# Holding the later loads of a fused attention and feed-forward kernel back until the second token tile's statistics are done

## The chip, the cores and the metric

The kernel runs on one core of a Trainium2 chip. The metric is the device time of one execution in microseconds (us); lower is better. Times are compared only within a job, that is, on one chip. Traces of different jobs come from different chips, so a difference between two of them can be one of the chips. In the engine names of the profile, PE is TensorE, PEld its weight loads, DVE is VectorE, ACT is ScalarE, POOL is GpSimd and SP is SyncE, which issues most of the DMAs.

## The reference, cut to what matters

Layer norm of 2048 tokens by 576 features, then linear attention (32 heads of 18) and a GEGLU feed-forward part (4608 wide) side by side on the same normalized input, both added to the input.

```python
x = A_x                                   # 1 x 2048 x 576, bf16
xn = _layernorm(x, axis=-1)
# attention: qkv = xn @ wqkv (576 x 1728); phi(q), phi(k); kv and z over all tokens; num / den; @ wo
# feed-forward: (gelu(xn @ w_gate) * (xn @ w_up)) @ w_down
return x + _A_ref(xn, A_wqkv, A_wo) + _B_ref(xn, B_w_gate, B_w_up, B_w_down)
```

Only the first 15 us matter here: the first token tiles of `x` and the K third of `wqkv` have to arrive, the tiles have to be normalized and transposed, and then TensorE can begin with the K projection and need not stop again for half a millisecond.

## The kernel before

The sixteen token tiles of `x` come in six loads, the K, Q and V thirds of the QKV weights in a load each, with a small load for the last 64 of their 576 rows. K goes through ScalarE's queue, everything else through SyncE's.

```python
def load_x(n0, cnt):
    nc.sync.dma_start(x_sb[:, n0:n0 + cnt, :], x_view[:, n0:n0 + cnt, :])

def load_w(which, on=nc.sync):
    c = slice(which * D, (which + 1) * D)
    on.dma_start(wqkv_sb[:, 0:4, c], A_wqkv[0:512, c].rearrange("(kt p) c -> p kt c", p=P))
    on.dma_start(wqkv_sb[0:HP, 4, c], A_wqkv[512:576, c])
    if which == 0:
        on.dma_start(wq_lo[HP:P, :], A_wqkv[512:576, c])
# ...
load_x(0, 1)
load_x(1, 1)
load_x(2, 2)
# ...
nc.vector.memset(wqkv_sb[0:1, 0, D:D + 2], 0.0)
load_w(1, nc.scalar)                      # K
```

The rest of the start is a list of steps, each with a time that only orders them. The statistics of tiles 0 and 1 stand at 3.15 and 4.09, the first normalization at 5.03. The loads of x 4 to 7, of the Q weights and of x 8 to 15 hang on a write of two elements into x tile 4: the load overwrites them, so SyncE has to wait for the write, and its queue is in order.

```python
todo += [(t, spin, count) for t, count in [(5.80, 3), (6.20, 5), (8.50, 2)]]   # filler matmuls

todo += [(4.0, lambda n: nc.vector.memset(x_sb[0:1, n, 0:2], 0.0), 4)]
todo += [(4.01, lambda n: load_x(n, 4), n) for n in (4,)]
todo += [(4.02, lambda n: load_w(0), 0)] + [(4.03, lambda n: load_x(n, 4), n) for n in (8, 12)]
todo.sort(key=lambda x: x[0])
```

`spin` multiplies an identity matrix by itself into an unused bank, so that TensorE is not idle between the first transposes.

## Time and profile before

| | before |
|---|---|
| time, median of the first 3 runs | 523.75 us (523.57 to 524.0) |
| span of the profiled run | 521.7 us, granted clock 1.0 |
| K weights issued, landed | 1.95, 7.37 us |
| TensorE's first K projection | 7.41 us, after 0.79 us of waiting |
| x 4 to 7: issue, first packet | 4.25, 5.66 us |

The lines behind this table stand in the prediction below. Where it or I speak of a first packet or of bytes at a time, they are counted from the trace's packet records by queue and packet size: packets of 4608 bytes are x 4 to 15, of 2304 bytes x 2 and 3, and q10 carries the K weights alone.

### The profile page before, as it was taken

The page shows a single profiled execution, that of the slowest core. Times are in us where ns is not written, and L with a number is a line of the kernel's source. Part 1 is how long each engine was busy: PE and PEld are TensorE (multiplying, and loading weights), DVE is VectorE, ACT ScalarE, POOL GpSimd, SP SyncE. Part 2 cuts the span into 40 slices and gives each one's busy share as a digit, 9 for nine tenths or more (in the row PEclk, how much of TensorE's full clock was granted, in tenths as well). Part 3 has the DMA queues.
Part 4 walks back from the last instruction along what each step waited for, and adds up shares of the span by engine and source line. Part 5 has one row for each costly group of instructions (what it writes and reads, how often), then busy time and mean ns, then how long its engine had stood idle before and what let it go on. Part 6 is the DMA issues. An engine that isn't in the chain of part 4 may idle for free.

```text
span 521.7 us, 10641 instructions
## 1 busy us (share of the span) xinstructions
PE 516.1 (99%) x4498; PEld 313.5 (60%) x4498; DVE 250.9 (48%) x436; ACT 143.1 (27%) x293; POOL 35.2 (7%) x55
## 2 busy tenths in 40 slices
PE   7999999999999999999999999999999999999997
PEld 6777755555587754444577744444777544445775
DVE  7996565876358323433388133333584233433101
ACT  6898442332320013323200032232000123322000
POOL 2021000211001100000012000000011000000000
PEclk9999999999999999999999999999999999999999
DMA  8334609899500045555300155555100355440000
GB/s 279 62 64 118 154 25 264 254 269 266 157 12 13 13 124 155 144 156 160 93 13 13 41 166 145 155 156 155 29 23 13 103 161 158 140 134 2 13 11 24
DMA packets 106282, 57.89 MB, mean 111 GB/s; under 512 B 13370, under 2 KB 105722, under 8 KB 106234
## 3 DMA queue, kind: packets, MB, share of 16 engines
q1 hardware_dynamic: 105626, 56.55, 38.8%
q8 instruction: 35, 0.57, 0.5%
q10 hardware_dynamic: 608, 0.66, 0.4%
q14 instruction: 13, 0.11, 0.1%
HBM read 52.86 MB, written 2.36 MB: 106 GB/s over the span
## 4 chain that ended last, share of the span: by engine, by line
PE 97%; DMA 1%; ACT 1%; DVE 0%; issue 0%
PE ps_all L313 55%; PE ps_all L677 27%; PE ps_all L289 4%; PE ps_all L682 4%; PE ps_all L245 3%; PE ps_all L342 3%; DMA wqkv_sb<-in_A_wqkv_dram 1%; PE ps_all L451 1%; PE ps_all L433 0%; PE ps_all L659 0%; ACT xnT L234 0%; ACT L114 0%; ACT phi_e L265 0%; ACT phi_e L269 0%; DVE hT L273 0%; DVE res L685 0%
## 5 line engine op out<-in xcount | busy, mean ns | idle before, releaser
L313 PE MATMUL ps_all<-xnT,wg 64*128 64x512 bf16 x1152 | 272.6, 376 | 0.0
L313 PE MATMUL ps_all<-xnT,wu 64*128 64x512 bf16 x1152 | 271.8, 376 | 0.0
L648 DVE TENSOR_TENSOR hT<-ps_all,gl 128x512 bf16<-128x512 f32 x144 | 99.5, 691 | 161.9 <-ACT gl L647 161.2
L647 ACT ACTIVATE gl<-ps_all 128x512 f32<-128x512 f32 x144 | 86.1, 598 | 314.3 <-PE ps_all L313 297.4
L313 PEld LDWEIGHTS <-wu 64*128 64x128 bf16 x1152 | 108.3, 94 | 66.3
L313 PEld LDWEIGHTS <-wg 64*128 64x128 bf16 x1152 | 108.3, 94 | 66.1
L677 PE MATMUL ps_all<-wd_sb,hT 128*128 128x288 bf16 x1152 | 147.0, 286 | 0.0
L677 PEld LDWEIGHTS <-hT 128*128 128x128 bf16 x1152 | 112.3, 98 | 30.6 <-issue 1.3
L475 DVE RECIPROCAL den_sb<-den_sb 126x128 f32<-126x128 f32 (+1 forms) x80 | 68.3, 911 | 0.5
L685 DVE TENSOR_TENSOR res<-ps_all,x_sb 128x288 bf16<-128x288 f32 x32 | 14.7, 458 | 88.0 <-PE ps_all L682 88.0
L313 PE MATMUL ps_all<-xnT,wr 64*128 64x512 bf16 x288 | 55.1, 376 | 0.0
L478 POOL TENSOR_TENSOR pqT<-pqT,den_sb 126x512 bf16<-126x512 bf16 (+3 forms) x25 | 24.2, 966 | 317.3 <-DVE den_sb L475 279.4
L682 PE MATMUL ps_all<-m_sb,pqT 126*128 126x288 bf16 (+1 forms) x160 | 24.9, 285 | 0.0
L313 PEld LDWEIGHTS <-wr 64*128 64x128 bf16 x288 | 14.4, 94 | 16.9 <-issue 0.7
L245 PE MATMUL ps_all<-wqkv_sb,xnT 128*128 128x288 bf16 x160 | 22.5, 286 | 0.9 <-DMA wqkv_sb<-in_A_wqkv_dram 0.8
L289 PE MATMUL ps_all<-hT,xn 128*128 128x288 bf16 (+4 forms) x176 | 22.4, 275 | 0.0
L289 PEld LDWEIGHTS <-xn 128*128 128x128 bf16 (+1 forms) x176 | 17.5, 102 | 4.1
L245 PEld LDWEIGHTS <-xnT 128*128 128x128 bf16 x160 | 15.4, 98 | 6.9 <-issue 1.4
L682 PEld LDWEIGHTS <-pqT 126*128 126x128 bf16 (+1 forms) x160 | 15.5, 97 | 4.1
L342 PE MATMUL ps_all<-xnT,wqkv_sb 128*126 128x512 bf16 (+1 forms) x70 | 17.4, 378 | 0.0
L273 DVE SCALAR_TENSOR_TENSOR hT<-ps_all,phi_e 128x288 bf16<-128x288 f32 x32 | 13.2, 450 | 4.6 <-ACT phi_e L269 4.0
L265 ACT ACTIVATE phi_e<-ps_all 128x288 f32<-128x288 f32 x32 | 12.9, 410 | 3.6 <-PE ps_all L245 2.1
(68 smaller groups left out, 173.8 us busy)
## 6 DMA issues: line engine op xcount, KB each, us to landing
wg<-in_B_w_gate_dram SPq DMA_DIRECT2D x72, 256.0 KB, 2.9
wu<-in_B_w_up_dram SPq DMA_DIRECT2D x72, 256.0 KB, 3.5
wd_sb<-in_B_w_down_dram SPq DMA_DIRECT2D x12, 432.0 KB, 4.6
wr<-in_B_w_gate_dram SPq DMA_DIRECT2D x72, 32.0 KB, 2.7
wr<-in_B_w_up_dram SPq DMA_DIRECT2D x72, 32.0 KB, 3.1
out_dram<-res SPq DMA_DIRECT2D x15, 144.0 KB, 1.8
x_sb<-in_A_x_dram SPq DMA_DIRECT2D x3, 576.0 KB, 7.1
wqkv_sb<-in_A_wqkv_dram SPq DMA_DIRECT2D x2, 576.0 KB, 4.7
```

Source lines behind the costliest of these rows:

```text
L245: nc.tensor.matmul(ps_all[:, k_bank(n, hf), :HALF], lhsT=xnT[:, kt, n * P:(n + 1) * P], rhs=wqkv_sb[:, kt, D + hf * HALF:D + (hf + 1) * HALF],
L273: nc.vector.scalar_tensor_tensor(out=out_, in0=ps, scalar=0.0, in1=e, op0=ALU.max, op1=ALU.add)
L289: nc.tensor.matmul(ps_all[:m, b, col:col + w], lhsT=xn[:, n, j0:j0 + m], rhs=pk[:, n, d0:d0 + w], start=(n == 0 and col == 0), stop=(n == ...
L313: return nc.tensor.matmul(self.outs[i], lhsT=self.lhs(i, rows, kt), rhs=self.rhs(i, rows, kt), start=start, stop=stop, skip_group_check=True,)
L342: nc.tensor.matmul(ps, lhsT=wqkv_sb[:, kt, q0:q0 + rows], rhs=xnT[:, kt, sc * SC:(sc + 1) * SC], start=(kt == 0), stop=(kt == KT - 1),)
L475: nc.vector.reciprocal(out=d[:, h:h + P], in_=d[:, h:h + P])
L478: nc.gpsimd.tensor_tensor(out=pqT[:rows, c, cols], in0=pqT[:rows, c, cols], in1=d, op=ALU.mult)
L647: nc.scalar.activation(out=gl[:], in_=ps_all[:, b[0], :], func=ACT.Gelu_apprx_tanh)
L648: nc.vector.tensor_tensor(out=hT[:, GUB * k + i, :], in0=ps_all[:, b[1], :], in1=gl[:], op=ALU.mult)
L677: nc.tensor.matmul(acc, lhsT=hT[:, f, j * P:(j + 1) * P], rhs=wd_sb[:, f, hs], start=(f == 0), stop=False,)
L682: nc.tensor.matmul(acc, lhsT=pqT[:rows, c, ts_], rhs=m_sb[:rows, c, hs], start=False, stop=(c == NCH - 1),)
L685: nc.vector.tensor_tensor(out=res[:, hs], in0=acc, in1=x_sb[:, n, hs], op=ALU.add)
```

## The change

The intent: the loads held back should come a microsecond later still, so that the K weights, which TensorE waits for, have the DMA engines to themselves.

```diff
-    todo += [(4.0, lambda n: nc.vector.memset(x_sb[0:1, n, 0:2], 0.0), 4)]
-    todo += [(4.01, lambda n: load_x(n, 4), n) for n in (4,)]
-    todo += [(4.02, lambda n: load_w(0), 0)] + [(4.03, lambda n: load_x(n, 4), n) for n in (8, 12)]
+    todo += [(5.0, lambda n: nc.vector.memset(x_sb[0:1, n, 0:2], 0.0), 4)]
+    todo += [(5.01, lambda n: load_x(n, 4), 4), (5.02, lambda n: load_w(0), 0)]
+    todo += [(5.03, lambda n: load_x(n, 4), n) for n in (8, 12)]
```

The write moves behind the second tile's statistics (4.09). No instruction is added or taken away on any engine, and only VectorE's order changes.

## The prediction

> **What bounds the kernel now.** I read the busy table and the chain of waits on the page first, then who waited for whom on TensorE, then the chain in order of time over the first 14 us, then the timelines of the engines there, and last the DMA queues in short stretches.
>
> From the page of the kernel before:
>
> ```profile
> PE 516.1 (99%) x4498; PEld 313.5 (60%) x4498; DVE 250.9 (48%) x436; ACT 143.1 (27%) x293; POOL 35.2 (7%) x55
> PE 97%; DMA 1%; ACT 1%; DVE 0%; issue 0%
> ```
>
> TensorE is busy for 99% of the span, and 97% of the chain that ended last is TensorE's own work. The 3% that is not (1% DMA, 1% ACT) is all a change to loads can reach. Who waited for whom on TensorE, over the whole run (what waited, for what: us in total, times, longest):
>
> ```profile
> PE ps_all L133 <- POOL ident masks.py:199: 1.4, 1, 1.4
> PE ps_all L245 <- DMA wqkv_sb<-in_A_wqkv_dram: 0.8, 1, 0.8
> PE ps_all L231 <- DVE xn L216: 0.3, 1, 0.3
> ```
>
> That is the whole list: three listed waits in 521.7 us, all in the first 8 us, and from 12 us on the same view is empty. So a microsecond gained or lost before 12 us should go through to the end nearly undiminished, and one lost later would have to be a new wait. The second line is the wait at stake: the first K projection waits 0.8 us for the K third of the QKV weights. The chain in order of time (start, length, what):
>
> ```profile
> 1.95 5.42 DMA wqkv_sb<-in_A_wqkv_dram
> 7.37 0.04 issue
> 7.41 0.79 PE ps_all L245 x5
> 8.20 0.02 issue
> 8.22 0.41 ACT phi_e L265
> 8.63 0.58 ACT xnT L234
> ...
> 11.53 0.47 DVE hT L273
> 12.00 0.04 issue
> 12.04 0.77 PE ps_all L245 x5
> ```
>
> The K weights are issued at 1.95 us, land at 7.37, and the matmuls begin 0.04 us later. Behind them the chain runs through ScalarE without a hole to 11.5 us, then hands over to TensorE at 12.04 for good. The start is therefore bound by one load, then by ScalarE's queue, which starts when that load lets it.
>
> Why does a load of 576 KB, plus a tail of 72 KB, take 5.4 us? In the queues, q10 carries only those two (608 packets, 0.66 MB on the page) and q1 the loads issued by SyncE. Between 5.5 and 6.0 us (queue, packets, MB, share of the 16 engines):
>
> ```profile
> q10 hardware_dynamic: 156, 0.16, 90.2%
> q1 hardware_dynamic: 9, 0.04, 29.6%
> ```
>
> and between 6.0 and 6.5 us:
>
> ```profile
> q1 hardware_dynamic: 25, 0.12, 81.3%
> q10 hardware_dynamic: 47, 0.04, 29.3%
> ```
>
> From one half microsecond to the next the K load drops from 0.16 MB to 0.04 MB, while the other queue takes over; another 13 packets of q10 trickle through from 6.5 to 7.0. What takes the engines is the load of x tiles 4 to 7 (576 KB in rows of 4608 bytes against the weights' 1152). It is held back by a 2-element write into its destination:
>
> ```profile
> 4.14 0.06 DVE L532 MEMSET x_sb<- 1x1 uint32 x1
> ```
>
> SyncE issues it right after, at 4.25 us; the first 4608-byte packets appear in the trace at 5.66 us, 1.4 us after the issue. The hold is too short: the K load then still has some 0.16 MB to go.
>
> **What the Trainium skill says.** "DMA: Bandwidth & Descriptors", section "Queues, rings and completion order", says that each DMA engine goes round the queue rows it has work for, a packet at a time. That is what the two stretches show: with 25 packets against 47, q1 took 0.12 MB against 0.04, since its packets are larger. The same page, section "Issuing engines are not separate DMA queues", says loads from different issuers interleave on the same 16 engines; the trace agrees, and so giving the K load ScalarE's queue did not protect it. "Perfetto Trace Analysis", section "Tensor Engine Instruction", says the end of a matmul in a profile is an estimate; hence I read TensorE's slack from what it waited for and from starts, not from ends.
>
> **The change part by part.** Nothing is added or removed. On every engine the instructions are the same; only on VectorE the 2-element write moves behind the second tile's statistics and their aggregation. Its own 0.06 us stays.
>
> 1. *When the held loads go.* VectorE before: write at 4.14, then two statistics, aggregation 4.97 to 5.18, then the first normalization at 5.10. After: the statistics come up to 0.05 us earlier, the write lands at about 5.1 and ends at about 5.15, and SyncE issues x 4 to 7 at about 5.2: **0.95 us later**. The Q weights, Q's extra copy and x 8 to 15 queue behind it and move by the same.
> 2. *When x 4 to 7 begins to move.* 5.66 + 0.95 = 6.6 us.
> 3. *When the K load ends without it.* By my count of q10's packets 512 of 648 KB were through by 5.75 us. It had run at 92 to 95 KB per quarter microsecond (0.19 MB in 5.25 to 5.75). The last 136 KB take 136 / 370 = 0.37 us: 6.1 us, and 6.2 to 6.3 for the engines that lag. That is before 6.6, so the delay is just long enough. From the last packet to the semaphore I see 0.40 us for x tiles 2 and 3 (last packet 5.24, landed 5.64) and 0.78 for the K tail (6.96, 7.74). So the K weights land at 6.5 to 6.9, estimate 6.75, against 7.37: **about 0.6 us earlier**, possibly 0.8.
> 4. *Whether TensorE can use it.* Its filler matmuls end at 6.62, so the start can move from 7.41 to 6.62 at the most: **0.79 us is the ceiling**. The first three transposed pieces of the tile are copied by 6.34 and the last two by 6.89 (VectorE's copy, 6.65 + 0.24). Those are the fourth and fifth matmuls, which a start at 6.75 reaches at about 6.75 + 3 x 0.155 = 7.2. So no loss there.
> 5. *Whether ScalarE can follow.* Relu of this half moves from 8.22 to about 7.57. The next transposed tile needs its normalized input: VectorE's second normalization is done at 7.22 and GpSimd's copy of its tail at 7.53, neither of which depends on the K load; its transposes can then be done by about 7.9, when Relu ends near 8.0. Further on the chain consists of what shifts along. I count the whole 0.6 to 0.7.
> 6. *What the later loads cost.* x 4 to 7 starts 0.95 us later but no longer shares with the K load: its 576 KB took from 5.66 to 8.58, 2.9 us, and alone at 350 KB per us would take 1.65 us plus stragglers. End about 8.7 to 9.0, landed about 9.4. VectorE reads tile 4 first at 10.35 now, some 9.65 after the shift. A slack of 0.2 us. The Q weights' tail landed at 11.54; up to 0.95 later is 12.5; the first Q unit starts at 13.48 now, 12.8 then. Slack 0.3, and more for the tail, which only the last of five matmuls reads. x 8 to 15 is wanted several us later.
>
> Sum: 0.65 us at 7.4 us, kept at 12 us, kept to the end, as TensorE has no waits there that could absorb it: 523.75 - 0.65 = **523.1 us**, 0.12%.
>
> **The rivals.**
>
> *A. The load lands sooner, but the wait moves to x.* If x 4 to 7 landed after 9.65, VectorE would wait for it, and the sum that frees TensorE at 12.04 comes after these statistics in VectorE's order. Against it is that the statistics, 1.06 us with their aggregation, ended at 11.41 while ScalarE used them only at 11.71, and the sum waited until 11.53. So there is some 0.1 to 0.3 us of room on top of the 0.2. If the load landed at 10.3 instead, half of the gain would be gone: about 523.4.
>
> *B. The K load is not slowed by sharing but by its own stragglers or by the receipt.* Packets fall off from 5.75 us, and 5.66 is when x begins; that coincidence speaks for sharing. But x tiles 2 and 3 too had trickled for a microsecond at their end, beside the K load. If the last engines were late for another reason, the weights would land at about 7.2: 523.55.
>
> *C. The delayed Q weights or the first DMA transposes become the wait.* The first transpose is issued at 12.97 and lands at 16.18 for matmuls at 16.99. It will be issued 0.65 sooner, while x 12 to 15 ends 0.5 to 0.9 later; more of both would overlap. With 0.8 us of room I give this 10%, with 523.4 to 523.9 as the result.
>
> *D. The gain is absorbed later.* Against it stands the empty list of TensorE's waits after 12 us.
>
> **Range and chances.** The ceiling of step 4 gives 523.75 - 0.79 = 522.96, and the three runs before spread over 0.43 us, so the low end is 522.65. B and C give 523.4 to 523.75; the high end is 523.65. Two per cent is 10.5 us, over ten times all that the start can give or lose; only a new state of the chip could reach it.
>
> **What would show it.** In the profile after: the 2-element write at about 5.1 and the issue at 5.2; q10 still above 0.1 MB between 5.75 and 6.25 and empty by 6.5; the K load landing at 6.5 to 6.9; TensorE's wait for it down from 0.79 to 0.1 or 0.2; the handover at about 11.4 instead of 12.04; no new wait on x or Q weights. A DMA wait before VectorE's statistics of tile 4 shows rival A, an unchanged landing B, a wait at the fourth tile's K projection C, and a handover that is earlier at an unchanged end D. The prediction is wrong if the handover does not move by about what the landing moves.

## The result, and the profile after

523.63 us median of 4 runs (523.31 to 525.36), against 523.66 for before with a fourth run. The ratio is 1.0006, 95% interval 0.9983 to 1.0028: the same. The predicted gain of 0.65 us is not there. The time lies just inside the predicted range, which says little, since the range reached nearly to the time before.

The run that was profiled is the one at 525.36. Its chain in order of time (start, length, what):

```profile
1.95 5.91 DMA wqkv_sb<-in_A_wqkv_dram
7.86 0.04 issue
7.90 1.31 PE ps_all L245 x5
```

The K weights land at 7.86 us, half a microsecond later than before, not 0.6 us earlier. The wait that was to shrink to 0.1 or 0.2 us has grown, and a wait for a transpose has joined it (TensorE's waits: total, times, longest):

```profile
PE ps_all L245 <- DMA wqkv_sb<-in_A_wqkv_dram: 1.4, 1, 1.4
PE ps_all L245 <- DMA xnT<-xn: 0.2, 1, 0.2
```

Also, the five matmuls of the first K projection take 1.31 us instead of 0.79. The view by stretches shows why (stretch, its length, TensorE busy, instructions, granted clock, DMA share, GB/s):

```profile
4.56:7.98 3.42, 1.80 (x25) 1.00 0.99 319
7.98:11.39 3.41, 3.41 (x22) 0.50 1.06 335
```

For exactly one stretch of 3.41 us TensorE ran at half clock, after a stretch in which it worked only 1.80 us of 3.42. From 11.39 on it is back at 1.00. So by the handover this run had lost 0.49 us to the later start and some 1.0 us more to the half clock (the handover matmuls start at 13.56 instead of 12.04).

Did the edit do what it was to do? The write and the issue are within 0.16 us of where I had put them (start, length, what):

```profile
4.94 0.06 DVE L532 MEMSET x_sb<- 1x1 uint32 x1
5.05 0.33 SPq L93 DMA_DIRECT2D x_sb<-in_A_x_dram  x1
```

That is 0.80 us later than the 4.25 of before. But the first packet of x 4 to 7 comes at 6.01 us, only 0.35 later than the 5.66 of before. And in the half microsecond from 6.0 to 6.5 the queues look like this (queue, packets, MB, share):

```profile
q10 hardware_dynamic: 141, 0.14, 81.9%
q1 hardware_dynamic: 10, 0.05, 70.9%
```

The K load still moves 0.14 MB here, where before it moved 0.04: in this run it is simply late. It was late before x 4 to 7 had sent a byte (at 5.75 us 359 of its 648 KB were through, against 513 before), so x 4 to 7 cannot be the reason for that part. One trace cannot tell what is. Hence the experiments.

### The profile page after: what moved, and what is told of

Same layout as the page of the kernel before. It is cut to its first block, busy times and chain, and to the rows that moved or that the text cites. A ratio compares the mean times of both kernels' runs of the same rounds, so it can differ in the third digit from the quotient of the medians.

```text
span 523.6 us, 10641 instructions
## 1 busy us (share of the span) xinstructions
PE 517.4 (99%) x4498; PEld 314.4 (60%) x4498; DVE 250.7 (48%) x436; ACT 143.4 (27%) x293; POOL 35.2 (7%) x55
## 4 chain that ended last, share of the span: by engine, by line
PE 97%; DMA 2%; ACT 0%; DVE 0%; issue 0%
PE ps_all L313 55%; PE ps_all L677 27%; PE ps_all L245 4%; PE ps_all L682 4%; PE ps_all L289 4%; PE ps_all L342 2%; DMA wqkv_sb<-in_A_wqkv_dram 1%; DMA xnT<-xn 1%; PE ps_all L451 1%; PE ps_all L433 0%; PE ps_all L659 0%; PE ps_all L231 0%; ACT L114 0%; DVE res L685 0%; ACT phi_e L265 0%; PE ps_all L422 0%
```

## The experiments

Four jobs of four, four, four and three kernels, and one of one. In all of them the output passed the comparison with the reference. "Before beside it" is the kernel before in the same job. "Slower" below means that its interval lies above 1, and for e3 and e4 it only touches 1. K's landing and the first packet of x 4 to 7 are of the one profiled run of each.

| run | what | x 4-7 issued | first packet | K landed | K projection starts | median us | before beside it | ratio, 95% interval |
|---|---|---|---|---|---|---|---|---|
| (first trace) | before | 4.25 | 5.66 | 7.37 | 7.41 | 523.66 | | |
| (first trace) | changed | 5.05 | 6.01 | 7.86 | 7.90 | 523.63 | 523.66 | 1.0006, 0.9983-1.0028 |
| e1 | before again | 4.20 | 5.89 | 7.54 | 7.58 | 523.62 | 523.62 | 1.0003, 0.9989-1.0016 |
| e2 | changed again | 5.09 | 6.19 | 7.83 | 7.87 | 523.84 | 523.62 | 1.0000, 0.9988-1.0013 |
| e12 | changed, third | 5.21 | 6.19 | 7.22 | 7.26 | 523.65 | 523.85 | 0.9993, 0.9981-1.0005 |
| e8 | no hold | 2.77 | 5.97 | 7.54 | 7.58 | 523.33 | 523.44 | 0.9996, 0.9984-1.0008 |
| e9 | hold 0.5 longer | 5.53 | 6.50 | 7.58 | 7.63 | 523.48 | 523.85 | 0.9990, 0.9978-1.0002 |
| e4 | hold 1.6 longer | 6.90 | 7.87 | 6.83 | 6.88 | 524.52 | 523.62 | 1.0013, 1.0000-1.0026 |
| e13 | the same, one look | 6.79 | 7.76 | 7.20 | 7.24 | 524.98 | 523.63 | one run |
| e3 | 12 more fillers | 5.18 | 6.16 | 7.29 | 7.33 | 524.24 | 523.62 | 1.0012, 1.0000-1.0025 |
| e6 | wide fillers | 5.24 | 6.21 | 7.35 | 7.39 | 523.91 | 523.44 | 1.0007, 0.9994-1.0020 |
| e5 | half the K load | 5.20 | 6.16 | 6.03 | 6.48 | 522.94 | 523.44 | 0.9986, 0.9974-0.9998 |
| e7 | before, less filler | 4.22 | 5.90 | 7.54 | 7.58 | 525.02 | 523.44 | 1.0022, 1.0006-1.0039 |
| e10 | hold 1.6 longer, split | 7.16 | 8.14 | 7.53 | 7.57 | 524.94 | 523.85 | 1.0026, 1.0009-1.0042 |
| e11 | no hold, half the K load | 2.77 | 5.14 | 6.87 | 6.91 | 523.89 | 523.85 | one run |
| e14 | x 2-3 behind K | 5.16 | 6.35 | 6.70 | 6.85 | 524.84 | 523.63 | one run |
| e15 | the same again | 5.16 | 6.29 | 6.61 | 6.65 | 525.68 | 523.63 | one run |
| e16 | x 3 behind K | 5.12 | 6.21 | 7.35 | 7.39 | 523.80 | 523.64 | 1.0009, 0.9995-1.0022 |

### Both kernels again, and a longer hold

e1 and e2 are the two kernels unchanged. e4 moves the write behind the first PSUM copy:

```diff
-    todo += [(5.0, lambda n: nc.vector.memset(x_sb[0:1, n, 0:2], 0.0), 4)]
+    todo += [(6.6, lambda n: nc.vector.memset(x_sb[0:1, n, 0:2], 0.0), 4)]
     # and the loads behind it from 5.01-5.03 to 6.61-6.63
```

> The kernel before, unchanged, for a second trace and for its spread. Theory T (the start's loads differ from run to run by some tenths of a us, and a start that leaves TensorE idle too long in one window is followed by a stretch at half clock): K weights land within 7.2 to 7.9 us, TensorE waits 0.6 to 1.3 us for them, clock 1.0 in most runs, times 523.4 to 524.0. Rival R1 (before is steady, the change itself makes the K weights late): they land within 0.1 of 7.37 again, all times within 523.4 to 524.0.

> The changed kernel, unchanged. Theory T: in a run without half clock the K weights land at 6.8 to 7.3, TensorE waits 0.2 to 0.7 us, time 523.2 to 523.5; now and then a run at 525 with clock 0.997. Rival R1 (the change itself makes them late): they land at 7.8 again, with a wait of 1.3 us, and half clock in more than a third of the runs. Rival R2 (x tiles 4 to 7 were never what held them back): they land at 7.3 to 7.5 as before, and the time is 523.5 to 523.7.

> The loads are held 1.6 us longer still (write at about 6.6, first packets of x 4 to 7 at about 8). If x 4 to 7 delays the K weights in the changed kernel too, they land at 6.7 to 6.9 here and TensorE's wait is 0.2 us; if not, they land as in the changed kernel (within the spread, 6.9 to 7.8). x 4 to 7 lands at about 10.8, about a us too late for VectorE, so a new DMA wait of 0.5 to 1.0 us before the statistics of tile 4, and a time of 523.5 to 524.5.

Before landed its K weights at 7.54 this time and the changed kernel at 7.83, all runs at a clock of 0.999 or more. TensorE's wait in the changed kernel, with no half clock in the run:

```profile
PE ps_all L245 <- DMA wqkv_sb<-in_A_wqkv_dram: 1.3, 1, 1.3
```

So a K load as late as that of the first trace does not always bring the half clock, and the half clock does not explain the late K load. The expected 6.8 to 7.3 is missed. At this point R1 (the change makes the K weights late) was alive; e3 (7.29 on the same chip, other filler only) and the third run e12 (below: 7.22) ended it.

e4 seemed to confirm the prediction's mechanism: with x 4 to 7 wholly out of the way the K weights landed at 6.83. But the kernel was rather slower all the same (1.0013, 1.0000 to 1.0026), by two waits of TensorE:

```profile
PE ps_all L245 <- DMA xnT<-xn: 0.7, 1, 0.7
PE ps_all L245 <- DVE hT L273: 0.7, 1, 0.7
```

The second is the late x 4 to 7, by way of VectorE, which waited 0.8 us for tile 4; the first is a DMA transpose that landed at 17.83 us instead of 16.18. The K projection started 0.53 us earlier than before, and by 17.9 us TensorE was 0.89 us behind. So a longer hold has a price of its own.

### More filler

```diff
-    todo += [(t, spin, count) for t, count in [(5.80, 3), (6.20, 5), (8.50, 2)]]
+    todo += [(t, spin, count) for t, count in [(5.80, 3), (6.20, 17), (8.50, 2)]]
```

> The changed kernel with 17 filler matmuls instead of 5 ahead of the first K projection, so TensorE works until about 7.2 us instead of 6.5. Theory T: no run with a clock below 1.0, highest time under 524.0; but the first K projection can't start before 7.2, so the fast runs gain nothing over the changed kernel (523.3 to 523.7). If the half clock has nothing to do with the idle time: runs at 525 come as often as without.

No run with a low clock, as expected, but 524.24 us: slower than expected by 0.5. In its chain of waits the K projection starts at 7.33, so nothing is lost there. The loss is further on (start, length, what):

```profile
24.85 4.29 DMA xnT<-xn
29.14 0.05 issue
29.18 0.91 PE ps_all L245 x6
```

A DMA transpose takes 4.29 us instead of the usual 2.6, and TensorE waits 0.5 us for it. In that time one packet of 16 KB passes on the queue of kind "instruction" (q8, from 26.98 us, 1.12 us long); in the kernel before it comes at 28.28, inside the next transpose, which takes 3.39. I took it for the fetch of further TensorE instructions, which comes earlier because 24 instructions were added, and which then meets another transpose. e6 tests that: the same number of instructions, but five of the fillers 512 columns wide.

```diff
-    todo += [(t, spin, count) for t, count in [(5.80, 3), (6.20, 5), (8.50, 2)]]
+    todo += [(t, spin, count) for t, count in [(5.80, 3), (8.50, 2)]] + [(6.20, spin_wide, 5)]
     # spin_wide: the same matmul with ident repeated four times as rhs
```

> The changed kernel with the same number of filler matmuls, but the five ahead of the K projection 512 columns wide instead of 128: TensorE works until about 7.4 us and no instruction is added. If the 0.65 us that the 12 added fillers cost came from the instruction fetch moved by 24 instructions (it then met another DMA transpose, and TensorE waited 0.5 us), this kernel shows no wait of TensorE for a transpose over 0.1 us, clock 1.0 in all runs, and 523.4 to 523.8. If the cost is that of the fillers themselves, 524.1 to 524.6 again.

The packet was at 28.28 us again, no wait of TensorE for a transpose is listed, and all five clocks were 1.0. The median of 523.91 lies above the expected 523.8 (two of the five runs were at 523.45 and 523.46, one at 524.62, and only one was traced). The profile agrees with the explanation, the spread of the times does not prove it.

### Is an earlier start worth anything?

e5 takes the wait itself away, by loading half of the K rows and using them twice.

```diff
-        on.dma_start(wqkv_sb[:, 0:4, c], A_wqkv[0:512, c].rearrange("(kt p) c -> p kt c", p=P))
+        nk = 2 if which == 1 else 4
+        on.dma_start(wqkv_sb[:, 0:nk, c], A_wqkv[0:nk * P, c].rearrange("(kt p) c -> p kt c", p=P))
 ...
-                rhs=wqkv_sb[:, kt, D + hf * HALF:D + (hf + 1) * HALF],
+                rhs=wqkv_sb[:, kt if kt == 4 else kt % 2, D + hf * HALF:D + (hf + 1) * HALF],
```

> The changed kernel, but the main K load brings 256 of the 512 rows (288 KB less) and the matmuls read them twice: a wrong result on purpose. It takes the wait for the K weights away whatever the other loads do. Theory C (a start earlier by d is d at the end, up to the ceiling of 0.8 us): K weights land at 6.2 to 6.6, TensorE starts at 6.5 to 6.6 with a wait under 0.2, and the time is 522.8 to 523.1. Rival (a floor set by the later x loads and transposes takes it back, as with the longer hold): the start is as early, but TensorE shows new waits between 11 and 30 us and the time is 523.4 to 523.9.

The result is wrong by construction; the comparison did not notice, so "passed" says little here about K. What counts is the time. The weights were there at 6.03 us and the filler set the start (start, length, what):

```profile
6.20 0.44 PE L134 MATMUL ps_all<-ident 128*128 128x128 bf16 x5
6.48 0.81 PE L246 MATMUL ps_all<-wqkv_sb,xnT 128*128 128x288 bf16 x5
```

TensorE's list of waits holds only the one at 1.4 us for the identity matrix. The start was 0.93 us earlier than in the first trace of before, and at 17 us TensorE was still 0.74 us ahead. The times: 522.97 mean against 523.67 in the same job, 0.70 us less. This is theory C of the expectation (not rival C of the prediction): what is gained at the start is kept to the end. Only the earlier start did not occur with the change.

### Without any hold

e8 is the opposite of the change: the write comes ahead of the first tile's statistics.

```diff
-    todo += [(4.0, lambda n: nc.vector.memset(x_sb[0:1, n, 0:2], 0.0), 4)]
+    todo += [(3.0, lambda n: nc.vector.memset(x_sb[0:1, n, 0:2], 0.0), 4)]
     # and the loads behind it from 4.01-4.03 to 3.01-3.03
```

> The write that holds the loads back comes before the first tile's statistics, so x 4 to 7 is issued at about 2.2 us instead of 4.2. If sharing the DMA engines with x 4 to 7 is what delays the K weights, they land at 8.6 to 9.5, TensorE waits over 2 us, the time is 524.8 to 526.5, in part at half clock. If they are late for reasons of their own, they land within 7.3 to 7.9 as in both kernels.

This run refuted the step on which the prediction stood, that the hold decides when x 4 to 7 moves. x 4 to 7 was issued at 2.77 us, 1.5 us earlier than before, and the K weights landed at 7.54 us as before. The queues from 5.25 to 5.75 us, when x 4 to 7 had been waiting for two and a half microseconds:

```profile
q10 hardware_dynamic: 161, 0.19, 110.5%
```

No packet of q1 at all. The first one of x 4 to 7 came at 5.97 us, 3.2 us after its issue. Neither the hold of before nor that of the change (first packets at 5.66 to 6.19) was what kept these tiles off the engines; only the longer holds of e9 and e4 did. And since x 4 to 7 began no earlier here, the run cannot tell what it costs the K load once it has begun.

What was? e11 combines no hold with half the K load (e5's edit on e8).

> No hold, and the main K load with 256 rows instead of 512 (wrong on purpose). If x 4 to 7 waits in a line behind the descriptors or packets of the K load, its first packet comes 0.8 to 1.2 us earlier than the 5.97 with the whole K load: at 4.8 to 5.2. If its start has a floor of its own, or hangs on x tiles 2 and 3, it stays at 5.7 to 6.0.

Its first packet came at 5.14 us, inside the expected 4.8 to 5.2. The same stretch, 5.25 to 5.75:

```profile
q1 hardware_dynamic: 32, 0.14, 90.5%
q10 hardware_dynamic: 77, 0.07, 42.3%
```

With 288 KB less of K weights ahead of them, the x tiles start 0.83 us earlier. So they wait in a line behind the K load, although they were issued on another queue (tiles 2 and 3 do the same when they are issued behind it, see e14). That explains the numbers of the table: the first packet comes either about 1.0 us after the issue (0.96 to 1.10 in every run issued at 5.05 or later, but 1.19 and 1.13 in e14 and e15, where tiles 2 and 3 were still moving on the same queue) or when the K load begins to thin out at 5.7 to 6.0 us, whichever is later.

But e11 shows something else too. Its half K load landed 0.8 us later than that of e5, where x 4 to 7 sent its first packet (6.16) only after the last of K (5.76). The issue lines of e5 and, after the dots, of e11:

```profile
wqkv_sb<-in_A_wqkv_dram ACTq DMA_DIRECT2D x1, 288.0 KB, 4.1
...
wqkv_sb<-in_A_wqkv_dram ACTq DMA_DIRECT2D x1, 288.0 KB, 4.9
```

From the moment when 136 KB were left, the K load took 0.69 us more in e5 and 1.32 in e11. That fits a cost of sharing, but it is one trace each, from two chips, and in e11 tiles 2 and 3 moved longer as well. The time gained nothing (523.89), since these tiles came 0.65 us late for VectorE.

### Half a microsecond longer, a split, and a third look

With the line known, a hold that ends just behind the K load ought to be best. e9 moves the write to 5.5; e10 takes e4's hold, but loads tiles 4 and 5 first and 6 and 7 behind the Q weights; e12 is the changed kernel a third time.

```diff
-    todo += [(5.0, lambda n: nc.vector.memset(x_sb[0:1, n, 0:2], 0.0), 4)]
+    todo += [(5.5, lambda n: nc.vector.memset(x_sb[0:1, n, 0:2], 0.0), 4)]      # e9
```

```diff
-    todo += [(6.61, lambda n: load_x(n, 4), 4), (6.62, lambda n: load_w(0), 0)]
+    todo += [(6.61, lambda n: load_x(n, 2), 4), (6.62, lambda n: load_w(0), 0), (6.625, lambda n: load_x(n, 2), 6)]   # e10, on e4
```

> The loads held 0.5 us longer than in the changed kernel (write behind the first normalization, issue at about 5.6). Theory Q (x 4 to 7 cannot send a packet before about 5.7 to 6.0 whatever its issue time, and otherwise does so 1.0 us after its issue): first packet at 6.6, K weights land at 6.8 to 7.1 as with the longest hold, x 4 to 7 lands at about 9.6, just in time; TensorE starts the K projection at 6.9 to 7.1 and the time is 523.0 to 523.2. Rival (only a hold past the whole K load helps): K weights at 7.3 to 7.8, time 523.4 to 523.8.

> The longest hold again, but x 4 to 7 split: tiles 4 and 5 first, tiles 6 and 7 behind the Q weights. If the late arrival of x 4 to 7 is what took the gain of the longest hold back, tile 4 lands at about 9.6 here, VectorE's wait of 0.8 us for it goes, the K weights land at 6.8 and the time is 522.9 to 523.3. If something else took it back (the transposes behind the late x 8 to 15), TensorE still waits 0.3 to 0.7 us for a transpose and the time is 523.6 to 524.5.

> The changed kernel a third time, for the spread. If it is no better and no worse than before: K weights at 7.2 to 7.9, TensorE's wait 0.6 to 1.4 us, median 523.4 to 523.9, and at most one run in five with a clock under 0.998.

e9's first packet came at 6.50 as expected, and yet the K weights landed at 7.58. The time is no worse and, within the interval, no better than before (0.9990, 0.9978 to 1.0002). e10 failed outright: 524.94 us (ratio 1.0026, 1.0009 to 1.0042). VectorE's wait for tile 4 was gone, as expected, but the K weights landed at 7.53 although nothing of x 4 to 7 was even issued before 7.16 us, and the first DMA transpose took 5.10 us, for which TensorE waited 1.1. The rival in the expectation was right in kind, though its wait (0.3 to 0.7) and its time (up to 524.5) were too small. e12 landed its K weights at 7.22, against 7.86 and 7.83 for the very same kernel, though on other chips.

### What the K load depends on

e13 repeats e4, and e14 (run twice, as e15) puts tiles 2 and 3 behind the K load:

```diff
-    load_x(2, 2)
 ...
-    nc.vector.memset(zrep[HP:P, NCH - 1, :], 0.0)
+    nc.vector.memset(zrep[HP:P, NCH - 1, :], 0.0); nc.vector.memset(x_sb[0:1, 2, 0:2], 0.0); load_x(2, 2)
```

> The longest hold again, for a second look at the K load without x 4 to 7 beside it. If the landing at 6.83 came from the hold, it is 6.7 to 6.95 again. If the landing spreads by itself over some 0.5 us, it is anywhere in 6.8 to 7.9, and 7.2 or more shows it. VectorE's wait of 0.5 to 0.9 us for tile 4 comes again in both.

> The changed kernel with x tiles 2 and 3 held until about 2.7 us, so that their load is issued behind the K load. If these tiles are what the K load shares with or waits behind, its first packet comes at about 3.0 instead of 3.9 and it lands at 6.0 to 6.7. If not, first packet 3.8 to 4.0 and landing 7.2 to 7.9. Tiles 2 and 3 then land at 6.5 to 7.5 and VectorE waits about 1 to 1.5 us for them, so the time is 524 to 525 either way.

> The same once more, since one look has shown a spread of half a microsecond: landing of the K weights within 0.3 us of the first, so at 6.0 to 6.9 if tiles 2 and 3 set it, at 7.2 to 7.9 if not.

e13 landed at 7.20, just on the bound that the expectation had set for a landing that spreads by itself. Its queues from 5.5 to 6.0 and, after the dots, from 6.0 to 6.5 and from 6.5 to 7.0:

```profile
q10 hardware_dynamic: 163, 0.17, 96.0%
...
q10 hardware_dynamic: 76, 0.07, 47.6%
...
q10 hardware_dynamic: 19, 0.01, 9.4%
```

Here nothing else is on the engines (x 4 to 7 starts at 7.76), and the K load still thins out over a microsecond: 0.17 MB, 0.07, then 0.01. It is the very shape (0.16, 0.04, 0.01) that I had read before as x 4 to 7 taking the engines away. The same loads up to this point gave 6.83, 7.20 and 7.53 (e4, e13, e10).

With tiles 2 and 3 behind it the K load changes clearly, and twice alike: first packet at 3.12 and 3.11 us instead of 3.9, landed at 6.70 and 6.61. Tiles 2 and 3, now issued at 2.77 us, sent their first packet at 5.48 and 5.43, as x 4 to 7 does behind the K load. The issue line of e14, to be set beside the 5.4 us from issue to landing of before (queue, count, size, time to landing):

```profile
wqkv_sb<-in_A_wqkv_dram ACTq DMA_DIRECT2D x1, 576.0 KB, 4.8
```

Tiles 2 and 3 landed 2 us later (7.71 and 7.60), TensorE waited 1.6 and 1.7 us for what hangs on them, and the times were 524.84 and 525.68. The second had a half clock again, after a stretch with 1.65 us of work:

```profile
9.35:12.76 3.41, 3.41 (x22) 0.50 1.07 364
```

The last run, e16, tries the middle: tile 2 ahead of the K load, tile 3 alone behind it.

```diff
-    load_x(2, 2)
+    load_x(2, 1)
 ...
-    nc.vector.memset(zrep[HP:P, NCH - 1, :], 0.0)
+    nc.vector.memset(zrep[HP:P, NCH - 1, :], 0.0); nc.vector.memset(x_sb[0:1, 3, 0:2], 0.0); load_x(3, 1)
```

> The changed kernel, with tile 2 ahead of the K load as before and tile 3 alone behind it. If the amount ahead of the K load sets its landing, it falls between 6.65 (neither tile ahead) and 7.5 (both): 6.8 to 7.2, first packet at about 3.5. Tile 3 then lands at about 7.0 to 7.6, VectorE wants it at about 7.0, so it waits up to 0.5 us. Time 523.1 to 523.5 if the K weights decide, 523.6 to 524.0 if tile 3 comes too late.

First packet of K at 3.54 as expected, but landed at 7.35 instead of 6.8 to 7.2, with tile 3 beside it, which landed at 8.00, 0.9 us too late for VectorE. 523.80 us against 523.64, ratio 1.0009 (0.9995 to 1.0022), one run of six at clock 0.997 and 525.65. No version found here beats both kernels.

### Too little filler

e7 is the kernel before without the eight fillers at 5.80 and 6.20, to see whether idle time brings the half clock.

```diff
-    todo += [(t, spin, count) for t, count in [(5.80, 3), (6.20, 5), (8.50, 2)]]
+    todo += [(t, spin, count) for t, count in [(8.50, 2)]]
```

> The kernel before without the eight filler matmuls around the first transposes (three and five). If a stretch with too little TensorE work is what is followed by 3.4 us at half clock, at least two of the five runs show a clock of 0.997 or lower and 524.7 to 525.6; runs without it stay at 523.4 to 524.2. If the half clock of the one changed run had another cause, all five runs are at 1.0 and 523.3 to 524.2.

Inconclusive: 525.02 us median, slower (ratio 1.0022, 1.0006 to 1.0039), but only one of six runs had a clock of 0.997 (525.43), and the traced one at 526.19 had lost its time elsewhere, to transposes and to a 1.4 us wait of TensorE for SyncE in the feed-forward part. Taking 16 instructions away had moved other things as well. The half clock comes without the change, too: one of the eleven runs of before in the third job had clock 0.997 and 525.47 us.

## Why the prediction was wrong

- **What bounds the kernel, and what a start is worth: right.** e5 gained 0.70 us from a start 0.93 us earlier and showed no new wait. A later start goes through as well: the traces of e1 and e2 start 0.17 and 0.46 us later than before, their handovers come later by just that, and their spans are 0.2 and 0.5 us longer. (e12 started 0.15 us earlier and handed over 0.15 earlier, but then waited 0.2 us for a transpose, and its span is 0.2 longer.)
- **The reading of the queues: the step that failed first.** "What takes the engines is the load of x tiles 4 to 7" rested on the two happening at once. The K load thins out by itself over the last microsecond, with nothing beside it (e13), and x 4 to 7 comes on because the K load is running out: with half the K load it comes 0.83 us earlier (e11), and issued 1.5 us earlier it does not come earlier at all (e8). That x 4 to 7 then costs the K load nothing is not shown (see Open). Rival B had this, with 7.2 us as its landing, and I dismissed it on the coincidence of two times. Nor do the two stretches show, as the prediction read them, that the engines go round the queues: the trace does not say which engine moved a packet, and in e8 x 4 to 7 got none through for 3.2 us after its issue.
- **Step 1, the issue: right but for a size.** 5.05 instead of 5.2, so 0.80 us later instead of 0.95.
- **Step 2, "5.66 + 0.95 = 6.6": wrong.** It took the 1.4 us from issue to first packet for a constant. About a microsecond is what such a load needs anyway (0.96 to 1.19 in the later issues), the rest was waiting behind the K load. The first packet moved by 0.35 us, to 6.01.
- **Step 3, landing at 6.75: wrong.** It let the last 136 KB take 0.37 us, and 0.45 to 0.55 us with the engines that lag. With nothing beside them they took 0.88, 1.04 and 1.12 us by my count of packets (e4, e13, e10), against 1.21 before: sharing can have cost 0.1 to 0.3 us there, not 0.6. The landings were 7.86, 7.83 and 7.22 for the changed kernel, 7.29 and 7.35 for the two that differ from it in filler only: mean 7.51. Before, again with e7: 7.37, 7.54, 7.54: mean 7.48. No difference, and a spread of 0.6 us in one kernel, as large as the gain I had worked out. The prediction took one trace's landing as the kernel's.
- **Step 6, the later loads: right for this change, and it is the price of more.** x 4 to 7 was in time in all traces of the changed kernel. With holds of 1.6 us more it was 0.8 and 0.9 us late (e4, e13).
- **Rivals A, C and D** did not occur with the change itself. A and C occurred with the longer holds. Transposes cost the changed kernel 0.2 us in two of its three traces, where one met a 16 KB instruction packet at 45 to 46 us.
- **The size of the whole effect.** Over all jobs the changed kernel's 14 runs at a clock of 0.999 or more have a mean of 523.64 us. For the 46 such runs of before beside the kernels it is 523.72 (for four of them the clock is not on record). That leaves no room for 0.65 us.
- **Two small sums** were off and changed nothing: 10.35 - 0.65 is 9.70, not 9.65, and 522.96 - 0.43 is 522.53, not 522.65.

**Open:** why a load thins out over its last microsecond, and why its landing differs by up to 0.6 us from trace to trace; the trace's packets do not say which engine moved them. Part of the difference is there before x 4 to 7 sends a packet: at 5.75 us 359 KB were through in the first changed trace, 536 in e4. Chips alone do not make it: e2 and e3, with the same loads on one chip, landed at 7.83 and 7.29. Open too whether x 4 to 7 costs the K load anything at all: without it the landings were 6.83, 7.20 and 7.53, mean 7.19, which is 0.3 us earlier than with it, from three looks with that spread; and the half K load landed at 6.03 without it and at 6.87 with it (e5, e11). The half K load with and without the hold, some traces each on one chip, would tell. And whether 1.8 us of work in a stretch decides on the half clock: 1.65 and 1.80 were followed by it, 1.94 and more were not, but e14 had one stretch with 1.80 that was not.

## What to carry to other kernels

Two loads that meet in time need not be in each other's way; before holding one back, issue it much earlier in a trial and see whether its own first packet moves (in e8 it did not), and look at the other load's end with nothing beside it (e13). Look at a second and third trace before treating a landing time as a property of the kernel: here one kernel spread as much as the predicted gain. And price what the load held back is itself needed for, since with 0.5 us more of holding it was in time (e9) and with 1.6 us more it was late (e4).

## What the Trainium skill lacked or had wrong

- "DMA: Bandwidth & Descriptors", section "Queues, rings and completion order": it says that an engine goes round the queue rows it has work for. It does not say that a load of one row may get no packet through while another row's load is under way. x 4 to 7, issued at 2.77 us, sent its first packet at 5.97 (e8), or 5.14 with half the K load (e11). What holds it back the traces do not show.
- The same page, section "Latency and other measured facts", gives about 600 ns to the first byte for DMAs from SyncE and ScalarE. Counted from the end of the issue the first changed trace agrees (5.38 to 6.01 us, 0.63), counted from its start it is 0.96 to 1.19 in the later issues. That it can become 3.2 us behind another load is not there.
- No page read here has a figure for the slow end of a load: with nothing beside it, the K load moved 0.07 MB in one half microsecond and 0.01 MB in the next (e13), after 0.19 MB from 5.25 to 5.75.
- "TensorE: Matmul & The Clock Gate", section "HAM oscillation — how this bites in real kernels": its rule is no idle gaps of TensorE above about 3.4 us. Here a gap of 1.40 us, with 1.80 us of work in the stretch of 3.42, was followed by one stretch of 3.41 us at 0.50. The length of that stretch agrees with the window that section "What's actually happening" gives.
- "Runtime: NRT & Kernel Launch", section "Instruction fetch mechanics", says that instructions are refilled in blocks of 16 KiB by DMA and that the cost of crossing from one to the next is mostly hidden. It does not say that a refill can meet a DMA transpose: here a packet of 16 KB on the queue of kind "instruction" lasted 1.12 us and lay inside a transpose that took 4.29 us instead of 2.6, for which TensorE waited 0.5 us (e3).
